# Keys of a group's two halves in the same columns, so that two blocks a group are turned instead of four

## The chip, the cores and the metric

The kernel runs on one core of one Trainium2 chip. The metric is the device time of one execution in microseconds, the median of several runs. A core has TensorE (PE in the profile), VectorE (DVE), ScalarE (ACT), GpSimd (POOL) and a sequencer that mostly issues transfers (SP), and 16 DMA engines that all queues share.

## What is computed

Two layers follow each other, for 8 batches of 3200 rows of 256 columns:

```python
# first layer: z is [B, S, 64], u and v are [B, S, 256]
scores = (1.0 / S) * np.matmul(z, z.transpose(0, 2, 1))
x = u * np.matmul(np.maximum(scores, 0.0) ** 2, v)
# second layer: w_q and w_k are [256, 64], w_out is [256, 256]
wq, wk = x @ w_q, x @ w_k
W_tok = (1.0 / np.sqrt(64)) * np.einsum('bsd,btd->bst', wq, wk)
out = np.maximum(np.einsum('bst,btd->bsd', W_tok, x), 0.0) @ w_out
```

The second layer has no function between its two products, so the kernel computes wk^T x first (a 64 x 256 matrix per batch, called heads here) and then wq times it, which avoids the S x S matrix.

## The kernel before

**Tiles and groups.** A batch's 3200 rows are 25 tiles of 128. They are worked off in 7 groups: six of 512 rows (4 tiles) and a last one of 128 rows (1 tile). For each group PE makes the scores of all 25 tiles against the group's rows (`scores`, L219, two tiles a time into the two banks of one PSUM tile), ACT or DVE takes max and scale (`first_stage`, L243 and L247), POOL or ACT squares (`second_stage`, L260 and L262), and PE accumulates the squares times v (`second_product`, L316). Since the scores are symmetric, some of them are not computed twice: blocks of squares are turned by a DMA transpose (L282) and used for another group. Most matmuls contract over 64 rows, and two of them run side by side, one on the upper 64 rows of the array, one on the lower; `top(r)` names these halves.

**From a finished group to its keys.** `gate` (L353) multiplies the accumulated product by u on DVE and writes x in fp16, laid out so that one DMA transpose (`turn_x`, L377) leaves the columns of tiles 0 and 1 of the group on the upper 64 rows and of tiles 2 and 3 on the lower. `projections` (L394) then multiplies by w_q and w_k together. The weights lie the other way round in the lower half: for tiles 0 and 1 (bank 0 of the PSUM tile) the queries come out on the upper rows and the keys on the lower; for tiles 2 and 3 (bank 1) the keys come out on the upper rows and the queries on the lower. `projections_out` (L407) copies both banks to an fp16 tile `qk` with one ACT copy of 128x512. `turn_keys` (L412) turns all four 128x128 blocks of `qk` by one DMA transpose on SP's queue into `kx`, of which `heads` (L421) uses the half with the keys. `mix` (L457) later multiplies the queries, which it reads from `qk` itself, by the heads of the batch; `proj` and `proj_stage` (L484, L509) multiply by w_out, and the output is stored (L563).

**What sets the order.** The kernel is unrolled and written out by a planner that runs while the program is built. It holds a clock for PE, DVE, ACT and POOL (`clock`), gives every piece of work a cost in microseconds (`give`), and decides by these clocks what PE issues next: second products (`acc_step`), a pair of scores (`use_pair`), or an extra such as keys, heads, mix or projection (`use_keys`, `use_heads`, `use_mix`, `use_proj`). Scores and extras need one of two PSUM slots (`slots`, tag `ps`), which stay closed until the planned end of the copy that empties them. DMA issues on SP are put in a list with a ready time, a due time, an issue cost and a cost on the DMA engines (`move`, `send`; a turned block costs 0.21 there); the ripe one that is due first is sent. The turn of keys becomes ready `SLACK` (1 us) after the copy and is due 10 us after it. Whether ACT or DVE does a first stage, and POOL or ACT a square, is the planner's choice by its clocks. `NAT` is the number of buffers for squares: a pair of tiles may only be made when the pair `NAT` before it has been used up; `lead` (140) sets how far ahead of the second products pairs are wanted.

**The tail.** The last batch's heads go another way for its last groups (`last_gram`, `last_heads`, L577 and L587). After the planned part some steps are written out by hand (L1077 to L1104), among them the projections of the last batch's groups 5 and 6 with their copies (L1096).

Of the kernel before, what the change touches and what calls it, by code (L numbers as in the profile page):

```python
# [9 lines left out]
FP16 = mybir.dt.float16  # L10
# [6 lines left out]
def kernel(  # L17
# [10 lines left out]
    nc = tc.nc  # L28
# [3 lines left out]
    dh = moe_w_q.shape[1]  # L32
    P = 128
# [3 lines left out]
    W = 512  # L37
    HW = W // 2
    widths = [512] * 6 + [128]
# [10 lines left out]
    ALPHA = C1 * float(S) * float(S)  # L50
    FINAL_SCALE = 1.0 / (8.0 * ALPHA * ALPHA * ALPHA)

    NAT = 15
    NX = 7
    NK = 5

# [5 lines left out]
    pk = ctx.enter_context(tc.tile_pool(name="pk", bufs=NK))  # L62
# [3 lines left out]
    psum = ctx.enter_context(tc.tile_pool(name="psum", bufs=2))  # L66
    pat = ctx.enter_context(tc.tile_pool(name="pat", bufs=NAT))
    ptt = ctx.enter_context(tc.tile_pool(name="ptt", bufs=1))
# [6 lines left out]
    def ps_tile(name):  # L75
        return pps.tile([P, 2, W], FP32, tag="ps", name=name)
# [5 lines left out]
    def top(r):  # L82
        return slice(r * dqk, (r + 1) * dqk)
# [3 lines left out]
    zT, vs, us, xs, xTs, qks, ks, hacc, hx, hss, rts, zds = ({} for _ in range(12))  # L87
# [294 lines left out]
    def x_rows(b, gi, n):  # L382
        return xs[b, gi][:, n % 2, :, n // 2, :]
# [3 lines left out]
    def halves(gi):  # L387
        return range((widths[gi] // P + 1) // 2)

    def projections(b, gi, ps):  # L390
        n = min(2, widths[gi] // P)
        for c in range(NC):
            for r in halves(gi):
                nc.tensor.matmul(  # L394
                    out=ps[:, r, 0 : n * P],
                    lhsT=wqk[top(r), c, :, :].rearrange("p t h -> p (t h)"),
                    rhs=xTs[b, gi][top(r), 0:n, c, :],
                    start=(c == 0),
                    stop=(c == NC - 1),
                )  # L400

    def projections_out(b, gi, ps):
        xTs.pop((b, gi))
        n = min(2, widths[gi] // P)
        qks[b, gi] = pq.tile([P, 2, HW], FP16, tag="qk", name="qk")
        nr = len(halves(gi))
        nc.scalar.copy(out=qks[b, gi][:, 0:nr, 0 : n * P], in_=ps[:, 0:nr, 0 : n * P])  # L407

    def turn_keys(b, gi):
        nn = widths[gi] // P  # L410
        ks[b, gi] = pk.tile([P, 4, 2, dh], FP16, tag="kx", name="kx")
        nc.sync.dma_start_transpose(  # L412
            out=ks[b, gi][:, 0:nn, :, :].rearrange("p n a h -> p n (a h)"),
            in_=qks[b, gi][:].rearrange("p r s -> p (r s)")[:, 0 : nn * P],
        )

    def heads(b, gis, ps):
        todo = [(gi, n) for gi in gis for n in range(widths[gi] // P)]
        for i, (gi, n) in enumerate(todo):
            for r in range(2):  # L420
                nc.tensor.matmul(  # L421
                    out=ps[top(i % 2), r, 0:D],
                    lhsT=ks[b, gi][top(r), n, 1 - n // 2, :],
                    rhs=x_rows(b, gi, n)[top(r), :, :],
                    start=(i < 2),
                    stop=(i >= len(todo) - 2),
                )
        for gi in gis:
            del xs[b, gi], ks[b, gi]
# [23 lines left out]
    def mix(b, gi, banks):  # L453
        n = min(2, widths[gi] // P)
        for db in range(ND):
            for r in halves(gi):
                nc.tensor.matmul(  # L457
                    out=banks[r][:, ds(db * n * P, n * P)],
                    lhsT=hss[b][top(r), ds(db * P, P)],
                    rhs=qks[b, gi][top(r), r, 0 : n * P],  # L460
                    start=(db == 0),
                    stop=(db == ND - 1),
                )
# [133 lines left out]
    PE, DVE, ACT, POOL = range(4)  # L597
    clock = [0.0] * 4
    FROM_PE, HOP = 0.27, 0.12

    def give(engine, ready, weight):
        clock[engine] = max(clock[engine], ready) + weight
        return clock[engine] + HOP
# [16 lines left out]
    def at_time(t, fn):  # L620
        later.append((t, fn))

    def move(ready, due, issue, takes, fn, landed=None, may=None):
        moves.append((ready, due, issue, takes, fn, landed, may))
# [29 lines left out]
    def open_slot():  # L654
        slot = slots.pop(0)
        assert slot[0] < 1e9
        clock[PE] = max(clock[PE], slot[0])
        slot[0] = 1e9
        slots.append(slot)
        return slot  # L660

    def close_slot(slot, t):
        slot[0] = t
# [40 lines left out]
    def use_keys(b, gi):  # L704
        slot = open_slot()
        ps = ps_tile("qk")
        projections(b, gi, ps)
        clock[PE] += 0.44 if gi < LASTG else 0.24
        ready = clock[PE] + FROM_PE
        projections_out(b, gi, ps)  # L710
        done = give(ACT, ready, 0.56)
        n = widths[gi] / P
        if b < last or gi < GRAM:
            move(
                done + SLACK, done + 10.0, 1.28, 0.21 * n, lambda: turn_keys(b, gi),
                lambda t: at_time(t, lambda: keys_landed(b, gi)), lambda: len(ks) < NK,
            )
        close_slot(slot, done)
# [3 lines left out]
    def keys_landed(b, gi):  # L722
        keyed.append((b, gi))
        for gis in FIRST_HEADS, range(3, NG if b < last else GRAM):
            if gi in gis and all((b, i) in keyed for i in gis):
                add_extra(clock[PE] + 0.5, "heads", lambda gis=gis: use_heads(b, gis))

    def use_heads(b, gis):
        slot = open_slot()
        ps = ps_tile("hd")  # L730
        heads(b, gis, ps)
        clock[PE] += 0.2 + 0.0547 * sum(widths[gi] // P for gi in gis)
        heads_out(b, ps)
        done = give(DVE, clock[PE] + FROM_PE, 0.7)
        close_slot(slot, done)
        if gis is FIRST_HEADS:
            return
        done = give(DVE, done, 0.35)
        move(done + SLACK, done + 2.0, 0.55, 0.1, lambda: cross_heads(b, 0))
        move(  # L740
            done + SLACK, done + 2.0, 0.55, 0.1, lambda: cross_heads(b, 1),
            lambda t: at_time(t, lambda: crossed(b)),
        )
# [16 lines left out]
    def use_mix(b, gi):  # L760
        slot = open_slot()
        ps = ps_tile("mx")
        mix(b, gi, [ps[:, 0, :], ps[:, 1, :]])
        clock[PE] += 0.22
        mix_out(b, gi, ps)
        done = give(ACT, clock[PE] + FROM_PE, 1.03 if gi < LASTG else 0.3)
        close_slot(slot, done)
        add_extra(done + 0.5, "proj", lambda: use_proj(b, gi))
# [91 lines left out]
    def x_landed(t, b, gi):  # L860
        if b < last or gi < LASTG - 1:
            add_extra(t + (XWAIT if b < last else 0.5), "keys", lambda: use_keys(b, gi))
# [100 lines left out]
    def p_chunk(p):  # L963
        t = [x[2] for x in tiles[2 * p : 2 * p + 2]]
        return max(c for c, (n0, nn) in enumerate(ZCH) for i in t if n0 <= i < n0 + nn) if p < 12 else 3

    def all_used(p):
        return all(x in used for x in tiles[2 * p : 2 * p + 2])
# [33 lines left out]
    while stages or work:  # L1002
# [17 lines left out]
        p = produced[0]  # L1020
        able = p < NPAIR and z_at[p_chunk(p)] <= now and (p < NAT or all_used(p - NAT) and turned_at.get(p - NAT, 0.0) <= now and not out_of.get(p - NAT))
        wanted = able and p * total < (done_acc[0] + lead) * NPAIR
# [40 lines left out]
    def mixed(b, gi, i=None):  # L1063
        if i is None:
            ps = ps_tile("mx")
            banks = [ps[:, 0, :], ps[:, 1, :]]
        else:
            ps = banks = [acc_tile(h, i % 2, "mx")[:] for h in range(len(halves(gi)))]
        mix(b, gi, banks)
        mix_out(b, gi, ps)  # L1070
# [22 lines left out]
    for gi in (LASTG - 1, LASTG):  # L1093
        ps = ps_tile("qq")
        projections(last, gi, ps)
        projections_out(last, gi, ps)  # L1096
# [38 lines left out]
```

## Time and profile before

| | us |
|---|---|
| median of 3 runs | 776.21 |
| the three runs | 772.63, 777.22, 776.21 |
| the profiled execution | 774.39 |
| its span, first to last instruction | 772.6 |
| granted TensorE clock, mean | 0.996 |

The profile has several views. The page gives busy time per engine, the span in 40 slices, the DMA queues, and the chain of work that ended last. The windows view gives for each stretch its length, then for PE, PEld (weight loads), DVE, ACT and POOL the busy time and number of instructions, then the granted clock, the DMA share and GB/s. The list of groups has one row for a line, engine, operation and shape: total busy time, mean nanoseconds of one, and the idle time before them with what ended it. The waits view has who waited for whom: total, times, longest. The timeline has instructions in order of time: start, length, engine, line and what ended an idle time before. A matmul's listed length is that of the whole passage through the array, so neighbouring ones overlap.

### The profile page before, as it was taken

What the parts mean: (1) busy time and instruction counts of PE and PEld (TensorE: products, weight loads), DVE (VectorE), ACT (ScalarE), POOL (GpSimd) and SP (SyncE); (2) the same over time, 40 slices, a digit from 0 to 9 for tenths busy, and PEclk for the clock granted to TensorE, in tenths of its full rate; (3) what the DMA queues carried; (4) which work ended last, traced back from release to release, by engine and by line L of the source; (5) the groups of instructions that cost most, each with busy time, mean ns of one, the idle gap of its engine ahead of it and who ended that gap; (6) DMA issues with size and microseconds to landing.
All of it is one profiled execution on the core that took longest, in us unless ns stands there. A gap on an engine that the chain in (4) does not pass through costs nothing.

```text
span 772.6 us, 28742 instructions
## 1 busy us (share of the span) xinstructions
PE 752.0 (97%) x12707; PEld 653.9 (85%) x12707; DVE 461.9 (60%) x497; ACT 496.9 (64%) x651; POOL 564.2 (73%) x363
## 2 busy tenths in 40 slices
PE   6999999999999999999999999999999999999996
PEld 3788889888888889988898898889988899888884
DVE  5775466555586365655556654755577656566644
ACT  6565666765676656777666666776657566775435
POOL 7996687885888477776788567875787768878740
PEclk9999999999999999999999999999999999999999
DMA  7999999999999999999999999999999999999536
GB/s 196 154 173 154 172 180 176 158 219 205 180 181 171 207 217 181 169 178 223 196 218 155 178 204 199 205 186 170 206 173 194 164 177 207 205 200 171 160 84 232
DMA packets 310094, 142.49 MB, mean 184 GB/s; under 512 B 287440, under 2 KB 291408, under 8 KB 309968
## 3 DMA queue, kind: packets, MB, share of 16 engines
q1 hardware_dynamic: 303056, 124.47, 88.9%
q0 software_dynamic: 6768, 15.98, 15.1%
q8 instruction: 99, 1.62, 0.9%
q14 instruction: 27, 0.22, 0.1%
q10 hardware_dynamic: 144, 0.20, 0.1%
HBM read 59.64 MB, written 26.21 MB: 111 GB/s over the span
## 4 chain that ended last, share of the span: by engine, by line
PE 93%; DMA 2%; DVE 2%; ACT 2%; issue 0%; POOL 0%; DVEq 0%; ACTq 0%
PE acc L316 68%; PE sc L224 13%; PE fo L509 5%; PE qk L394 3%; PE hd L421 2%; PE mx L457 1%; DVE g L247 1%; DMA tt<-at 1%; DMA v_sb<-in_v_dram 1%; PE fo L484 1%; ACT g L243 1%; ACT at L260 0%; DMA z<-in_z_dram 0%; ACT rt L472 0%; PE xtx L577 0%
## 5 line engine op out<-in xcount | busy, mean ns | idle before, releaser
L262 POOL TENSOR_TENSOR at<-g 128x1024 f16<-128x1024 f32 (+1 forms) x279 | 520.2, 1880 | 171.7 <-DVE g L247 123.5
L316 PE MATMUL acc<-v_sb,at 64*128 64x256 f16 x7312 | 493.7, 269 | 3.7 <-DMA v_sb<-in_v_dram 2.3
L247 DVE TENSOR_SCALAR g<-sc 128x1024 f32<-128x1024 f32 (+1 forms) x292 | 348.5, 1207 | 214.0 <-PE sc L224 198.1
L316 PEld LDWEIGHTS <-at 64*128 64x128 f16 x7312 | 386.7, 94 | 57.6 <-issue 4.6
L243 ACT ACTIVATE g<-sc 128x1024 f32<-128x1024 f32 (+2 forms) x176 | 173.1, 988 | 118.1 <-PE sc L224 106.8
L260 ACT ACTIVATE at<-g 128x1024 f16<-128x1024 f32 (+2 forms) x189 | 191.1, 1019 | 18.3 <-DVE g L247 14.7
L224 PE MATMUL sc<-zT 64*128 64x512 f16 x920 | 175.8, 378 | 2.9 <-DVE g L247 2.0
L316 PE MATMUL acc<-v_sb,tt 64*128 64x256 f16 x2304 | 167.4, 269 | 1.7 <-DMA tt<-at 1.3
L316 PEld LDWEIGHTS <-tt 64*128 64x128 f16 x2304 | 123.9, 94 | 18.3 <-DMA tt<-at 1.6
L353 DVE TENSOR_TENSOR x_sb<-acc,u_sb 128x512 f16<-128x512 f32 x92 | 59.1, 684 | 26.2 <-PE acc L316 23.1
L562 ACT ACTIVATE fo<-fo 128x1024 f32<-128x1024 f32 (+2 forms) x44 | 42.7, 980 | 37.3 <-PE fo L509 33.3
L224 PEld LDWEIGHTS <-zT 64*128 64x128 f16 x920 | 55.3, 94 | 13.0 <-issue 8.3
L474 ACT ACTIVATE rt<-mx 128x1024 f16<-128x1024 f32 (+1 forms) x49 | 44.7, 929 | 17.1 <-PE mx L457 17.0
L509 PE MATMUL fo<-wo,rt 64*128 64x256 f16 x668 | 52.2, 269 | 0.2 <-DVE g L247 0.2
L407 ACT CAST qk<-qk 128x512 f16<-128x512 f32 (+1 forms) x54 | 29.2, 540 | 25.5 <-PE qk L394 25.3
L509 PEld LDWEIGHTS <-rt 64*128 64x128 f16 x668 | 36.1, 94 | 3.3 <-issue 0.4
L303 ACT COPY sign<-sign 1x1 f32<-1x1 f32 x95 | 17.3, 182 | 33.1 <-PE acc L316 31.2
L394 PE MATMUL qk<-xT_sb,wqk 64*128 64x256 f16 (+1 forms) x404 | 31.6, 265 | 0.0
L316 PE MATMUL acc<-v_sb,ttl 64*128 64x256 f16 x384 | 27.2, 269 | 0.0
L394 PEld LDWEIGHTS <-wqk 64*128 64x128 f16 x416 | 22.3, 94 | 2.0 <-issue 0.3
L316 PEld LDWEIGHTS <-ttl 64*128 64x128 f16 x384 | 20.5, 94 | 2.7
L526 DVE COPY sign<-sign 1x1 f32<-1x1 f32 x31 | 4.4, 142 | 29.9 <-PE fo L509 29.7
(54 smaller groups left out, 203.7 us busy)
## 6 DMA issues: line engine op xcount, KB each, us to landing
u_sb<-in_u_dram SPq DMA_DIRECT2D x48, 512.0 KB, 4.9
out_dram<-fo SPq DMA_DIRECT2D x45, 512.0 KB, 3.9
v_sb<-in_v_dram POOLq DMA_DIRECT2D x35, 320.0 KB, 6.0
zn<-in_z_dram POOLq DMA_DIRECT2D x7, 400.0 KB, 6.2
tt<-at SPq DMA_TRANSPOSE x144, 4.7
out_dram<-fo SPq DMA_DIRECT2D x6, 256.0 KB, 2.4
u_sb<-in_u_dram SPq DMA_DIRECT2D x8, 128.0 KB, 3.6
hx<-ha SPq DMA_DIRECT2D x16, 64.0 KB, 4.0
```

The source lines that it names most:

```text
L224: nc.tensor.matmul(out=sc[:, h, 0:gw], lhsT=zT[b][top(h), ts(ti, P)], rhs=zT[b][top(h), ds(gs, gw)], start=True, stop=True,)
L243: nc.scalar.activation(out=g[:, hs, 0:w], in_=sc[:, hs, 0:w], func=RELU, scale=GSCALE)
L247: nc.vector.tensor_scalar(out=g[:, hs, 0:w], in0=sc[:, hs, 0:w], scalar1=0.0, scalar2=GSCALE, op0=AOP.max, op1=AOP.mult,)
L260: nc.scalar.square(out=out, in_=g[:, hs, 0:w])
L262: nc.gpsimd.tensor_mul(out=out, in0=g[:, hs, 0:w], in1=g[:, hs, 0:w])
L316: product = nc.tensor.matmul(out=g["acc"][k][:, ds(j * D, D)], lhsT=weights(b, gi, ti, 2 * k + j if whole else 0)[top(r), :], rhs=vs[b][to ...
L353: nc.vector.tensor_mul(out=out, in0=g["acc"][k][:].rearrange("p (m d) -> p m d", d=dh), in1=u2.rearrange("p n (c d) -> p (n c) d", d=dh),)
L394: nc.tensor.matmul(out=ps[:, r, 0 : n * P], lhsT=wqk[top(r), c, :, :].rearrange("p t h -> p (t h)"), rhs=xTs[b, gi][top(r), 0:n, c, :], st ...
L407: nc.scalar.copy(out=qks[b, gi][:, 0:nr, 0 : n * P], in_=ps[:, 0:nr, 0 : n * P])
L474: nc.scalar.activation(out=out, in_=ps[:, 0:nr, 0 : ND * n * P], func=RELU)
L509: product = nc.tensor.matmul(out=ps[:, bank, ds(j * D, D)], lhsT=flat[top(r), ds((dc * n + j) * P, P)], rhs=wo[top(r), dc, :], start=(stag ...
L562: nc.scalar.mul(out=flat_out[:, sl], in_=part, mul=FINAL_SCALE)
```

## The change

The single ACT copy becomes two copies of 64 rows, one for the upper and one for the lower half, and the second writes its two banks in reverse order. So in a full group slot 0 of `qk` holds the queries of both halves and slot 1 the keys of both halves. The transpose takes slot 1 alone, two blocks instead of four, and `kx` has half the size. `heads` and `mix` read the new places. The last, small group copies its one block to slot 1. Both copies of a group go to the same engine, ACT or DVE, whichever the planner's clocks call free first; in the hand-written tail they stay on ACT. The planner costs the pair at 1.17 us (0.3 for the small group) where it had 0.56, and the turn at half of what it was on the DMA engines. `NAT` goes from 15 to 16.

```diff
-    NAT = 15
+    NAT = 16
...
-    def projections_out(b, gi, ps):
+    def projections_out(b, gi, ps, on_act=True):
         xTs.pop((b, gi))
         n = min(2, widths[gi] // P)
         qks[b, gi] = pq.tile([P, 2, HW], FP16, tag="qk", name="qk")
-        nr = len(halves(gi))
-        nc.scalar.copy(out=qks[b, gi][:, 0:nr, 0 : n * P], in_=ps[:, 0:nr, 0 : n * P])
+        copy = nc.scalar.copy if on_act else nc.vector.tensor_copy
+        if widths[gi] == W:
+            copy(out=qks[b, gi][top(0), :, :], in_=ps[top(0), :, 0 : n * P])
+            copy(out=qks[b, gi][top(1), ::-1, :], in_=ps[top(1), :, 0 : n * P])
+        else:
+            copy(out=qks[b, gi][:, 1, 0 : n * P], in_=ps[:, 0, 0 : n * P])
...
     def turn_keys(b, gi):
-        nn = widths[gi] // P
-        ks[b, gi] = pk.tile([P, 4, 2, dh], FP16, tag="kx", name="kx")
+        nn = min(2, widths[gi] // P)
+        ks[b, gi] = pk.tile([P, 2, 2, dh], FP16, tag="kx", name="kx")
         nc.sync.dma_start_transpose(
             out=ks[b, gi][:, 0:nn, :, :].rearrange("p n a h -> p n (a h)"),
-            in_=qks[b, gi][:].rearrange("p r s -> p (r s)")[:, 0 : nn * P],
+            in_=qks[b, gi][:, 1, 0 : nn * P],
         )
...
-                    lhsT=ks[b, gi][top(r), n, 1 - n // 2, :],
+                    lhsT=ks[b, gi][top(r), n % 2, 1 - n // 2, :],
...
-                    rhs=qks[b, gi][top(r), r, 0 : n * P],
+                    rhs=qks[b, gi][top(r), 0 if widths[gi] == W else 1, 0 : n * P],
...
         ready = clock[PE] + FROM_PE
-        projections_out(b, gi, ps)
-        done = give(ACT, ready, 0.56)
-        n = widths[gi] / P
+        takes = 1.17 if widths[gi] == W else 0.3
+        on_act = max(clock[ACT], ready) < max(clock[DVE], ready)
+        projections_out(b, gi, ps, on_act)
+        done = give(ACT if on_act else DVE, ready, takes)
+        n = min(2, widths[gi] // P)
```

## The prediction

> **What bounds the kernel now.** I read the page first: busy time, the slices, the DMA queues and the chain that ended last.
>
> ```profile
> span 772.6 us, 28742 instructions
> ...
> PE 752.0 (97%) x12707; PEld 653.9 (85%) x12707; DVE 461.9 (60%) x497; ACT 496.9 (64%) x651; POOL 564.2 (73%) x363
> ...
> DMA  7999999999999999999999999999999999999536
> DMA packets 310094, 142.49 MB, mean 184 GB/s; under 512 B 287440, under 2 KB 291408, under 8 KB 309968
> q1 hardware_dynamic: 303056, 124.47, 88.9%
> HBM read 59.64 MB, written 26.21 MB: 111 GB/s over the span
> PE 93%; DMA 2%; DVE 2%; ACT 2%; issue 0%; POOL 0%; DVEq 0%; ACTq 0%
> ```
>
> Two resources look full: PE, busy for 97% of the span, and the DMA engines, nine tenths in nearly every slice. The chain decides: 93% of it is PE and 2% DMA. ACT (64%) and DVE (60%), which the change loads, have room on average. Next I split the span in start, body and tail with the windows view, and asked whom PE waits for in the body.
>
> ```profile
> 0.00:20.00 20.00, 12.45 (x117) 7.89 (x119) 11.01 (x13) 12.85 (x14) 15.36 (x23) 0.91 0.78 193
> 20.00:740.00 720.00, 714.45 (x12270) 626.41 (x12266) 437.14 (x467) 470.15 (x610) 544.82 (x336) 1.00 1.08 185
> 740.00:772.60 32.60, 25.09 (x331) 19.58 (x325) 13.77 (x19) 13.87 (x29) 3.99 (x6) 0.95 0.50 167
> ```
>
> ```profile
> PE sc L224 <- DVE g L247: 1.6, 3, 1.0
> PE acc L316 <- DMA tt<-at: 1.3, 1, 1.3
> PE acc L316 <- POOL at L262: 0.7, 1, 0.7
> ```
>
> In the windows the first number after the stretch is its length, the second PE's busy time; a wait has its total, its times and its longest. In the body PE is idle for 720.00 - 714.45 = 5.55 us; start and tail have 7.55 and 7.51 us. Of the body's idle time only 1.3 us is put down to a transfer, in one wait. The DMA share of 1.08 there (queues overlapping on the same engines) costs PE almost nothing as the order stands.
>
> Busy PE can hide short gaps, since one matmul's 0.269 us covers the next one's start. So I worked out how much PE time the matmuls need when they stream.
>
> ```profile
> 745.43 3.00 PE L316 MATMUL acc<-v_sb,at 64*128 64x256 f16 x52
> L316 PE MATMUL acc<-v_sb,at 64*128 64x256 f16 x7312 | 493.7, 269 | 3.7 <-DMA v_sb<-in_v_dram 2.3 <-POOL at L262 0.7 <-ACT sign L303 0.4
> L316 PE MATMUL acc<-v_sb,tt 64*128 64x256 f16 x2304 | 167.4, 269 | 1.7 <-DMA tt<-at 1.3 <-DVE x_sb L353 0.3
> L316 PE MATMUL acc<-v_sb,ttl 64*128 64x256 f16 x384 | 27.2, 269 | 0.0
> L224 PE MATMUL sc<-zT 64*128 64x512 f16 x920 | 175.8, 378 | 2.9 <-DVE g L247 2.0 <-ACT g L243 0.2
> L509 PE MATMUL fo<-wo,rt 64*128 64x256 f16 x668 | 52.2, 269 | 0.2 <-DVE g L247 0.2
> L394 PE MATMUL qk<-xT_sb,wqk 64*128 64x256 f16 (+1 forms) x404 | 31.6, 265 | 0.0
> L457 PE MATMUL mx<-qk,hs 64*128 64x256 f16 (+1 forms) x208 | 19.8, 266 | 0.5 <-ACT qk L407 0.5
> L421 PE MATMUL hd<-x_sb,kx 64*64 64x256 f16 x382 | 13.9, 273 | 0.0
> L484 PE MATMUL fo<-wo,rt 128*128 128x256 f16 x66 | 8.5, 273 | 1.4 <-DVE fo L557 1.3
> ```
>
> Row one: 52 matmuls, two at a time on the two halves of the rows, take 3.00 us, of which the last pair's 0.27; (3.00 - 0.27) / 25 = 0.109 us a pair. The 256-column groups have (7312 + 2304 + 384 + 668 + 404 + 208) / 2 = 5640 pairs, 615 us; the scores 460 pairs of twice the columns, 100 us; heads 13.9 us; the tail's projections (L484) 8.5 and three smaller groups some 6 us. Together about 744 us. So 772.6 - 744 = 28.6 us of the span is not streaming, 20.6 of it the visible idle time and about 8 hidden. The change adds and removes no matmul, so it can gain at most 5.55 + 8 = 13.6 us in the body, and only where a wait goes; 7.7 us are 1%.
>
> **The change part by part.** *The second copy.* One copy of 128x512 per full group becomes two of 64 rows by 512 columns each, both on the engine that the planner calls free first.
>
> ```profile
> L407 ACT CAST qk<-qk 128x512 f16<-128x512 f32 x47 | 27.4, 583 | 24.9 <-PE qk L394 24.7
> L434 DVE COPY ha<-hd 128x512 f32<-128x512 f32 x8 | 5.5, 689 | 4.0 <-PE hd L421 3.9
> L189 POOL CAST wqk<-wk 64x256 f16<-64x256 f32 x2 | 0.8, 406 | 0.0
> L120 POOL CAST zd<-z 128x384 f16<-128x384 f32 x1 | 0.5, 498 | 1.5 <-DMA z<-in_z_dram 1.5
> L120 POOL CAST zd<-z 128x448 f16<-128x448 f32 x1 | 0.6, 570 | 0.0
> ```
>
> No row has 64 rows by 512 columns on ACT or DVE. If the time went with the rows, a copy would cost half of 0.583 = 0.29 us and the pair nothing more than now; if it goes with the columns, 0.583 on ACT and, by the nearest DVE row that reads PSUM, 0.689. The only casts with 64 rows are POOL's: 0.406 us for 256 columns, while its 128-row casts fall by 0.072 us per 64 columns, to about 0.35 at 256. Half the rows were no cheaper, so I take the upper end: the pair costs 1.17 us on ACT (+0.58) and 1.38 on DVE (+0.80 over the old copy; 0.21 over the planner's 1.17). With 48 full groups that is 28 to 38 us more work on two engines that are idle for some 276 and 311 us. [...]
>
> What lies on the path? Until both copies are done, one of the two score slots (the PSUM pair "ps") stays shut 0.6 to 0.8 us longer, and ACT or DVE starts its next item later. PE's cover is the second product, which needs no slot: the planner chooses it when no slot is open. The cover is missing where no row of it is ready; today's price for that is the row PE sc <- DVE g, 1.6 us in 3 waits. Bounds for the body: 0 if all is covered, 46 x 0.6 = 28 us if none is (of the 47 copies in the row above one is in the tail); near the lower end by that row, I take +1.0 us. Behind a copy on DVE stand the next L247 and the gate L353; behind one on ACT the next L243, L260, sign L303. The planner moves both clocks by 1.17, so only DVE's 0.21 is unknown to it; at most 24 copies x 0.21 = 5 us, counted within those bounds. The keys themselves are not urgent: they are due 10 us after the copy, and SP's transpose is sent 1 us (SLACK) after the planned end, which holds DVE's 0.21. If that cover went, SP would stand, with the loads of u and the turned blocks behind it.
>
> *The turn.* 12 blocks fewer in each of 7 batches and 8 in the last: 92 blocks of 128x128.
>
> ```profile
> L412 SPq DMA_TRANSPOSE kx<-qk x53: 1123/1275/3088, 68.5 to 735.5; - x53
> 83.64 0.61 PE L316 MATMUL acc<-v_sb,tt 64*128 64x256 f16 x8 [1.34 <-DMA tt<-at]
> ```
>
> The number of transposes stays 53, and SP's issue time falls little: one-block turns are among these 53, yet the shortest is 1.123 us against a median of 1.275, so up to 0.15 us each, 8 us of SP's time in all, on no path that PE shows. The DMA work of a block: the program turns about 2110 blocks (1344 of the products, 400 of x, 191 of keys, 175 of z), 287440 small packets, 136 a block. Queue 1's packets average 0.889 x 772.6 x 16 / 303056 = 36 ns, so 136 x 36 / 16 = 0.31 us at most (large packets raise that mean), and 0.21 in the planner. 92 blocks are 19 to 28 us of DMA time, 2.5 to 3.7%. On PE's path it can return what PE waits for transfers in the body: 0 to 1.3 us seen. I take -1.3, the one late turned block, since it falls at 83.6 us, when key turns are running (from 68.5 us). [...]
>
> *The planner.* Turns are costed at half, pairs may run 16 instead of 15 ahead (NAT), and the copies move between ACT and DVE. NAT rarely decides: the lead of 140 products lets pairs run 140 x 460 / 5000 = 13 ahead of the mean. I cost it at nothing, within the body's bounds: the 13.6 us above as gain, and as loss some waits of the kind listed, like the longest now (1.3 us) a few times. The order after the first key copy will differ nearly everywhere. The other edits (heads and mix read other columns of the same tiles, the small group's copy stays one of 128x128) issue the same instructions as before: nothing, with one answer.
>
> *The tail.* Here PE has no second product to hide behind.
>
> ```profile
> 750.77 0.59 ACT L407 CAST qk<-qk 128x512 f16<-128x512 f32 x1
> 751.40 0.39 PE L457 MATMUL mx<-qk,hs 64*128 64x256 f16 x4 [0.46 <-ACT qk L407]
> 751.73 2.14 PE L577 MATMUL xtx<-xd 128*128 128x256 f16 x18
> 756.19 0.75 ACT L407 CAST qk<-qq 128x512 f16<-128x512 f32 x2 [0.89 <-PE qq L394]
> 756.83 2.21 ACT L472 ACTIVATE rt<-mx 128x512 f16<-128x512 f32 x4
> ```
>
> At 751.4 PE already waits 0.46 us for group 4's copy, and everything after stands behind it in order: +0.6 (ACT) to +0.8 (DVE). At 756.19 the copies of groups 5 and 6 stay on ACT; the first becomes two, and the four activations that PE's last products need start directly behind: +0.59. Bounds 0 (time by rows) to 1.4; I take +1.2.
>
> **Sum.** +1.0 - 1.3 + 0 + 1.2 = +0.9 us. The profiled execution took 774.39 us (1.8 outside its span) and lies 1.8 below the median of the three runs, 776.21, inside their 772.63 to 777.22. 774.4 + 0.9 = **775.3 us**.
>
> **Rivals.**
> *The slot becomes the bound (slower).* The longer hold makes PE wait before the next scores where all ready rows of the second product are used up. For: PE has already 3 such waits of up to 1.0 us, and two slots serve scores, keys, heads, mix and projections. Against: PE's idle time before the scores is 1.6 us in 720. It decides from about 13 of the 46 copies exposed (13 x 0.6 = 8 us); with 20, +12: 786 us.
> *The freed DMA time pays (faster).* Turned blocks land earlier, rows are ready earlier and the gaps close. For: the DMA share of 1.08 in the body. Against: one DMA wait of 1.3 us. All visible idle time of the body gone: 774.4 + 1.2 - 5.55 = 770; over 1% needs about 4 us of the hidden as well: 766 us.
> *The turn does not get cheaper.* If a transpose's time goes by instruction and not by block, the -1.3 is lost and the copies remain: 774.4 + 2.2 = 776.6 us. For: the narrow spread of issue times, 1.123 to 1.275. Against: 136 packets for each block.
>
> **How the numbers follow.** The forecast 0.46; the turn not cheaper 0.22; the slot 0.24; DMA pays 0.08. A measurement of this kernel can tell about 1% from no change (its own three runs spread 0.6%). Forecast and dearer turn lie within 1% of 774 to 776: 0.68; slower 0.24; faster 0.08. The range reaches down to 768, between the two ends of the DMA rival, and up to 785, just under the slot rival's price, since half of that rival's cases are milder than its 20 exposed copies; some 0.05 is left out below and 0.13 above.
>
> **What would show it.** Copies: two L407-like rows per group, 64x512, 0.58 on ACT and 0.69 on DVE; 0.29 would mean time by rows. Turn: kx transposes still 53, small packets down by 92 x 136 = 12500, DMA share of the body down by 0.03. Body: PE idle near 5 us, waits of sc for g or qk still under 3 us; 10 us or more is the slot rival. Tail: the stretch from 740 longer by about a microsecond. I am wrong if PE's idle time in the body falls by several microseconds, or if it grows in places that no copy touches: then the planner's new order did it, a term that I set to nothing.

## The result, and the profile after

The changed kernel takes 782.82 us (median of 6 executions) against 775.77 for the kernel before in the same comparison: 1.0085 times as long, 95% interval 1.0055 to 1.0114. The forecast was 775.3 us, no change; the change is a small loss. Executions more than 1.5% above the fastest one of the same kernel are left out of the ratios and ranges here (794.91 us of the change, 785.71 of e3, 789.66 of e4, four of e9 from 788.9 to 789.6, and 2786.82 of e8), so that the spreads of the change, e3, e4 and e9 are if anything larger than given.

The executions of the changed kernel lie far apart, from 776.6 to 786.5 us; those of before lie within 5 us. The profiled execution is the fastest one, 776.62 us with a span of 774.5, 1.9 us longer than the span of before, so most of the loss is not in it. The page of after, the three windows and PE's waits in the body:

```profile
span 774.5 us, 28772 instructions
...
DMA packets 298317, 139.47 MB, mean 180 GB/s; under 512 B 275664, under 2 KB 279632, under 8 KB 298192
...
q1 hardware_dynamic: 291280, 121.46, 83.3%
```

```profile
0.00:20.00 20.00, 13.11 (x105) 8.01 (x106) 10.95 (x13) 12.05 (x13) 15.30 (x23) 1.00 0.77 189
20.00:740.00 720.00, 714.34 (x12264) 617.92 (x12265) 471.02 (x525) 464.46 (x589) 556.39 (x347) 1.00 1.03 181
740.00:774.50 34.50, 25.81 (x343) 20.12 (x338) 13.93 (x19) 14.39 (x29) 4.25 (x6) 0.95 0.47 157
```

```profile
PE sc L224 <- DVE g L247: 2.8, 5, 0.8
PE mx L463 <- DVE g L247: 0.6, 1, 0.6
...
PE sc L224 <- DVE qk L409: 0.2, 1, 0.2
```

The DMA work fell: 11776 small packets fewer (92 blocks of 128; the prediction had counted 136 a block), queue 1 from 88.9 to 83.3% of the span, the body's DMA share from 1.08 to 1.03 (0.03 was forecast), and the 1.3 us wait for a turned block is gone. PE shows no gain from it: its idle time in the body is 5.66 us where it was 5.55. So 5.6 points less of queue 1's share bought no time that shows. What the copies cost, in the list of groups of after by shape:

```profile
L408 DVE CAST qk<-qk 64x512 f16<-64x512 f32 x36 | 24.6, 682 | 28.7 <-PE qk L394 28.6
L409 DVE CAST qk<-qk 64x512 f16<-64x512 f32 x36 | 25.0, 695 | 0.5
L408 ACT CAST qk<-qk 64x512 f16<-64x512 f32 x11 | 6.4, 578 | 6.2 <-PE qk L394 6.1
```

The time goes with the columns, not the rows: 0.68 and 0.70 us on DVE and 0.58 on ACT are the times of 128 rows of 512 columns (0.69 on DVE in e4, 0.58 on ACT in before), while the small group's 128 rows of 128 columns took 0.29 on DVE and 0.26 on ACT in this trace. 36 of the 47 planned pairs went to DVE, 1.38 us each where the planner counts 1.17. PE's wait for a copy's slot in the body is one of 0.2 us.

So this trace shows the copies hidden in the body, the turns halved, and a span 1.9 us longer, of which the tail has 1.2 (shown further down). The rest of the loss had to be looked for in the order of the work and in slower executions.

### The profile page after: what moved, and what is told of

The parts are those of the page before. It is cut to its first block, busy times and chain, and to the rows that moved or that the text cites. A ratio compares the mean times of both kernels' runs of the same rounds, so it can differ in the third digit from the quotient of the medians.

```text
span 774.5 us, 28772 instructions
## 1 busy us (share of the span) xinstructions
PE 753.3 (97%) x12707; PEld 646.0 (83%) x12707; DVE 495.9 (64%) x555; ACT 490.9 (63%) x629; POOL 575.9 (74%) x375
## 3 DMA queue, kind: packets, MB, share of 16 engines
q1 hardware_dynamic: 291280, 121.46, 83.3%
## 4 chain that ended last, share of the span: by engine, by line
PE 92%; DVE 3%; ACT 1%; issue 1%; DMA 1%; POOL 0%; DVEq 0%; ACTq 0%; POOLq 0%
PE acc L316 67%; PE sc L224 13%; PE fo L515 5%; PE qk L394 3%; DVE g L247 2%; PE hd L427 2%; PE mx L463 1%; DMA v_sb<-in_v_dram 1%; PE fo L490 1%; ACT at L260 0%; DMA z<-in_z_dram 0%; ACT g L243 0%; PE xtx L583 0%; ACT rt L478 0%; POOL at L262 0%
## 5 line engine op out<-in xcount | busy, mean ns | idle before, releaser
L262 POOL TENSOR_TENSOR at<-g 128x1024 f16<-128x1024 f32 (+1 forms) x291 | 532.1, 1845 | 160.1 <-DVE g L247 107.0
L247 DVE TENSOR_SCALAR g<-sc 128x1024 f32<-128x1024 f32 (+1 forms) x277 | 329.7, 1205 | 148.3 <-PE sc L224 136.9
L243 ACT ACTIVATE g<-sc 128x1024 f32<-128x1024 f32 (+2 forms) x191 | 188.1, 990 | 125.3 <-PE sc L224 120.5
L260 ACT ACTIVATE at<-g 128x1024 f16<-128x1024 f32 x177 | 183.1, 1042 | 28.6 <-DVE g L247 25.8
L224 PE MATMUL sc<-zT 64*128 64x512 f16 (+1 forms) x920 | 180.5, 380 | 4.1 <-DVE g L247 3.2
L316 PE MATMUL acc<-v_sb,tt 64*128 64x256 f16 x2304 | 164.1, 269 | 0.0
L408 DVE CAST qk<-qk 64x512 f16<-64x512 f32 x36 | 24.6, 682 | 28.7 <-PE qk L394 28.6
L316 PE MATMUL acc<-v_sb,ttl 64*128 64x256 f16 x384 | 29.2, 269 | 0.0
L409 DVE CAST qk<-qk 64x512 f16<-64x512 f32 x36 | 25.0, 695 | 0.5
```

The lines of the kernel that those rows point to most:

```text
L224: nc.tensor.matmul(out=sc[:, h, 0:gw], lhsT=zT[b][top(h), ts(ti, P)], rhs=zT[b][top(h), ds(gs, gw)], start=True, stop=True,)
L243: nc.scalar.activation(out=g[:, hs, 0:w], in_=sc[:, hs, 0:w], func=RELU, scale=GSCALE)
L247: nc.vector.tensor_scalar(out=g[:, hs, 0:w], in0=sc[:, hs, 0:w], scalar1=0.0, scalar2=GSCALE, op0=AOP.max, op1=AOP.mult,)
L260: nc.scalar.square(out=out, in_=g[:, hs, 0:w])
L262: nc.gpsimd.tensor_mul(out=out, in0=g[:, hs, 0:w], in1=g[:, hs, 0:w])
L316: product = nc.tensor.matmul(out=g["acc"][k][:, ds(j * D, D)], lhsT=weights(b, gi, ti, 2 * k + j if whole else 0)[top(r), :], rhs=vs[b][to ...
```

## Experiments

Ratios are against the kernel before on the same chip, with 95% intervals. Two theories stood at first: that the second copy holds the PSUM slot and PE waits for it (the copies), and that the planner's new order is worse (the order). The program's order can be held fixed while the work is changed, since the planner decides by its own costs; e2 has the order of before on PE, SP and POOL, and e4 that of e3, but for the size of the key turns.

**e1_again: the changed kernel once more.**

> The changed kernel once more, for its spread and a second trace. Both theories: 1.006 to 1.012 times the time before. Theory of the order (the planner's new order of work brings waits that differ from one execution to the next): spans from about 774 to 784 us again, far wider than the 5 us of the kernel before. Theory of the copies (the second copy of each group holds its PSUM slot 0.6 to 0.8 us longer, and PE waits for it): the same excess in every execution, so a narrow spread.

Measured 784.0 us, 1.0146 (1.0114 to 1.0178), 781.1 to 789.5. The wide spread is there again, and the loss is larger. Its trace has a span of 779.0 us, and waits that the first trace of after does not have or has much shorter (there 1.3 us for the exchange, 0.6 for mix, none of PE for keys or x):

```profile
DVE hs L454 <- DMA hx<-ha: 5.3, 2, 4.2
PE mx L463 <- DVE g L247: 3.2, 2, 2.5
PE hd L427 <- DMA kx<-qk: 1.0, 1, 1.0
PE qk L394 <- DMA xT_sb<-x_sb: 0.7, 1, 0.7
```

```profile
20.00:740.00 720.00, 709.68 (x12180) 615.00 (x12176) 467.62 (x522) 459.81 (x581) 551.28 (x345) 1.00 1.03 181
```

PE is idle for 10.3 us in this body, 4.8 more than in before, and PE's three waits above add up to 4.9. None of them is for a copy of queries and keys.

The timeline of the longest: the two transfers that exchange the halves of the heads, DVE's sum that needs them, the first stages behind it, and PE's mix.

```profile
233.11 2.14 SPq L156 DMA_TRANSPOSE zT<-zd  x1
235.34 1.18 SPq L449 DMA_DIRECT2D hx<-ha  x2
240.80 0.43 DVE L454 TENSOR_TENSOR hs<-ha,hx 128x256 f16<-128x256 f32 x1 [4.24 <-DMA hx<-ha]
241.14 2.35 DVE L247 TENSOR_SCALAR g<-sc 128x1024 f32<-128x1024 f32 x2
242.41 0.39 PE L463 MATMUL mx<-qk,hs 64*128 64x256 f16 x4 [2.50 <-DVE g L247]
```

The sum stands in DVE's queue ahead of the landing; DVE is idle for 4.24 us, no first stage frees a slot, and PE waits 2.50 us. DVE had come to the sum at 236.6 us, 1.2 us after the exchange was issued. In the first trace of after, the same sum of the same program does not wait:

```profile
230.92 1.23 SPq L156 DMA_TRANSPOSE zT<-zd  x1
232.24 1.48 SPq L449 DMA_DIRECT2D hx<-ha  x2
235.58 0.92 DVE L454 TENSOR_TENSOR hs<-ha,hx 128x256 f16<-128x256 f32 x1
```

There the exchange went out 3.1 us earlier. In e1 it stood behind transposes on SP's queue whose issue took longer (the last of them 2.14 us against 1.23). In the kernel before, the same pair of rows is 7.4 us apart and nobody waits:

```profile
236.39 1.18 SPq L443 DMA_DIRECT2D hx<-ha  x2
243.82 0.41 DVE L448 TENSOR_TENSOR hs<-ha,hx 128x256 f16<-128x256 f32 x1
```

**e2_old_order: the work of the change in the order of before.**

```diff
-    NAT = 16
+    NAT = 15
...
-        on_act = max(clock[ACT], ready) < max(clock[DVE], ready)
-        projections_out(b, gi, ps, on_act)
-        done = give(ACT if on_act else DVE, ready, takes)
-        n = min(2, widths[gi] // P)
+        projections_out(b, gi, ps)
+        done = give(ACT, ready, 0.56)
+        n = widths[gi] / P
```

> The work of the change in the order of before: two copies of 64 rows (all on ACT) and two turned blocks, but the planner's costs and NAT of before, so every engine issues in the order of before, with one more ACT copy per full group. Theory of the order: 0.997 to 1.003, of which 1 us is the tail's two longer copies. Theory of the copies: 1.006 or more, since the longer hold is not even planned for.

Measured 787.58 us, 1.0174 (1.0160 to 1.0188), all four executions within 0.7 us. The copies do cost time where the planner doesn't know of them. Its waits, and one of them:

```profile
PE sc L224 <- ACT qk L409: 5.9, 21, 0.7
```

```profile
138.83 0.71 PE L316 MATMUL acc<-v_sb,at 64*128 64x256 f16 x10
139.19 0.58 ACT L409 CAST qk<-qk 64x512 f16<-64x512 f32 x1
139.83 0.39 PE L224 MATMUL sc<-zT 64*128 64x512 f16 x2 [0.28 <-ACT qk L409]
```

The ten products before the scores stream for 5 x 0.109 = 0.55 us, so the scores could start at 139.38; they start at 139.83. The list shows 0.28 us of these 0.45, since the products' last passage covers the rest. At that size, 21 such waits make 9.5 us of the 13.5, an estimate; eight waits of PE for the same copy before other work list 2.1 us, and the tail's two copies make 1.2 more.

**e3_nat15 and e4_new_order_old_work: one order, both kinds of work.** The first is the change with NAT 15. The second has its order, but one copy of 128x512 and four turned blocks:

```diff
-        nc.scalar.copy(out=qks[b, gi][:, 0:nr, 0 : n * P], in_=ps[:, 0:nr, 0 : n * P])
+        copy = nc.scalar.copy if on_act else nc.vector.tensor_copy
+        copy(out=qks[b, gi][:, 0:nr, 0 : n * P], in_=ps[:, 0:nr, 0 : n * P])
...
-        projections_out(b, gi, ps)
-        done = give(ACT, ready, 0.56)
-        n = widths[gi] / P
+        takes = 1.17 if widths[gi] == W else 0.3
+        on_act = max(clock[ACT], ready) < max(clock[DVE], ready)
+        projections_out(b, gi, ps, on_act)
+        done = give(ACT if on_act else DVE, ready, takes)
+        n = min(2, widths[gi] // P)
```

> The change with NAT at 15 instead of 16. If the 16th buffer is what changes the order for the worse: within 0.3% of before. If the order is bad for the costs of the copies and turns: 1.005 to 1.012, as the change. Theory of the copies: 1.008.

> The order of the kernel with NAT 15 and the planner's new costs, but with the work of before: one copy of 128x512 (on the engine that this order gives it) and four turned blocks. PE, SP and POOL issue in the same order as in that kernel. Theory of the order: 1.005 to 1.012, like the kernel with NAT 15. Theory of the copies: 0.997 to 1.003, since the copy is short again.

Measured 1.0034 (1.0011 to 1.0057), 773.9 to 784.4, and 1.0045 (1.0018 to 1.0071), 774.3 to 784.4. With the order the same, the second copies and the halved turns together change nothing that can be told; these two runs do not separate a cost of the one from a gain of the other. The old work in a new order is slower than before and spreads just as widely. The theory of the copies falls for planned copies. The excess is a little below what the theory of the order had said; the rest came with NAT 16, the only thing in which e1 (1.0146) differs from e3.

**What in the order?** The planner puts a consumer where it expects its transfer to have landed: the end of its DMA clock plus 4.0 us (LANDS). The change halves the cost of a key turn in that clock. Running the planner of each kernel gives its own figures: from issue to expected landing x takes 8.0 us before and 7.3 after, all SP transfers 7.55 and 7.30. The measured medians did not follow for x:

```profile
xT_sb<-x_sb SPq DMA_TRANSPOSE x56, 4.8
```

```profile
xT_sb<-x_sb SPq DMA_TRANSPOSE x56, 5.2
```

(before, then after). For the keys both went down, the planner's figure from 6.9 to 6.7 us and the measured median from 4.7 to 4.2. For the exchange of the heads the planner's figure went up, from 5.9 to 6.3, so the long wait of e1 does not come from an earlier expected landing of the exchange itself; it went out late, as shown above. So a second theory was put against chance: work is planned closer to its transfers (the DMA clock), or any order other than that of before costs as much (any new order).

**e5_turn_at_four and e6_lands_5: the change with honest or later landings.** In e5 `n = min(2, widths[gi] // P)` in `use_keys` goes back to `n = widths[gi] / P`; in e6 `LANDS = 4.0` becomes 5.0.

> The change, except that the planner goes on costing a turn of keys at four blocks (0.84 us) on the DMA engines, though two are turned. Theory of the DMA clock (with the turn at half, the planner expects transfers to land earlier than they do, and puts the work that needs them, above all DVE's sum of the heads after the exchange, ahead of the landing): 0.998 to 1.004, and the time from the issue of the heads' exchange to DVE's sum back from 2.4 to 8 us to 4.6 us and more, as before. Theory of any new order (an order other than the one of before costs about as much whatever changed it): 1.005 to 1.015.

> The change, with the planner expecting every SP transfer to land 5.0 us after its place in the DMA clock instead of 4.0. Theory of the DMA clock: 0.998 to 1.005 and a spread near that of before. Theory of any new order: 1.005 to 1.015.

Measured 1.0030 (1.0011 to 1.0049), 774.6 to 780.2, and 1.0024 (1.0004 to 1.0044), 772.9 to 779.7. One number in the planner takes back most of the loss, though on another chip than e1's; on e1's chip e14 has 1.0044. But e5's trace still has one long wait for the exchange, whose sum DVE reached 1.6 us after the issue, so its distances were not back as far as expected. It also shows what came with that wait:

```profile
146.13 0.43 DVE L454 TENSOR_TENSOR hs<-ha,hx 128x256 f16<-128x256 f32 x1 [4.76 <-DMA hx<-ha]
147.75 0.61 PE L224 MATMUL sc<-zT 64*128 64x512 f16 x2 [3.13 <-DVE g L247]
```

```profile
146.00:149.00 3.00, 1.16 (x8) 0.57 (x9) 2.87 (x4) 1.14 (x2) 0.10 (x1) 0.74 1.08 259
149.00:152.00 3.00, 3.00 (x38) 2.57 (x37) 1.21 (x2) 1.13 (x2) 3.00 (x2) 0.69 1.04 208
152.00:155.00 3.00, 3.00 (x58) 2.89 (x55) 2.17 (x3) 2.08 (x4) 2.54 (x2) 1.00 1.28 193
```

From 146 to 152 us, with the end of PE's pause in it, the granted clock is 0.74 and then 0.69, and PE gets through 38 matmuls in 3 us where it does 58 at 1.00. If the fall belongs to the pause, this late transfer cost more than the wait that the list puts down to it. For the 2.50 us wait in e1 no such fall is to be seen in the clocks: the first 20 us have 0.91 and the stretch from 740 us on 0.96 in both traces, and the mean of the whole execution is 0.996 in e1 and 0.994 in e5, where 6 us at 0.7 make some 0.002, an estimate.

**e7_before_turn_at_two and e8_before_copy_060: the kernel before with one planner number moved.** e7 halves the cost of the turn, e8 moves the copy's 0.56 to 0.60; all work is that of before.

> The kernel before, all its work kept (one copy on ACT, four turned blocks), only the planner's cost of the turn on the DMA engines halved. Theory of the DMA clock: 1.005 to 1.015 with a wide spread, since the planner's clock runs ahead of the transfers. Theory of the copies: no change, 0.998 to 1.002. Theory of any new order: 1.003 to 1.015 as well, so this run alone doesn't tell these two apart; the next one does.

> The kernel before, all its work kept, only the planner's cost of the key copy on ACT moved from 0.56 to 0.60 us, which changes the order without touching the DMA clock's costs. Theory of the DMA clock: 0.998 to 1.003 and a narrow spread. Theory of any new order: 1.003 to 1.015.

Measured 1.0049 (1.0023 to 1.0075), 775.1 to 785.0, and 1.0050 (1.0026 to 1.0073), 777.7 to 781.1. The medians do not tell the theories apart: a neutral change of order costs 0.5% too, against the expectation. The spreads do: 9.9 us against 3.4 (of 12 and 6 executions). And only e7's trace has PE waiting for a transfer:

```profile
PE hd L421 <- DMA kx<-qk: 1.7, 1, 1.7
```

**e9_sum_on_pool: the late sum out of DVE's queue.** `nc.vector.tensor_add` of the heads' sum becomes `nc.gpsimd.tensor_add`, in the order of the change.

> The change in its own order, except that the sum of the heads after their exchange is added by POOL and not by DVE, so that a late exchange no longer stands ahead of the first stages in DVE's queue (it then stands ahead of the squares in POOL's). Theory that this one wait makes most of the excess and the spread: 1.001 to 1.006, with the spread halved. Theory that the order places many things too close to the transfers: 1.008 to 1.015, as the change.

Measured 1.0070 (1.0040 to 1.0099), 775.2 to 783.6. That wait is one of several, not most of it. The trace, of an execution of 788.91 us, has many:

```profile
PE hd L427 <- DMA kx<-qk: 9.8, 6, 4.7
```

**e10_old_order_one_copy and e11_new_order_one_copy: halved turns without a second copy.** A full group's projections write queries and keys to their places at once, and one copy of 128x512 moves both banks; e10 also has e2's edits of `NAT` and of the planner's costs:

```diff
-            for r in halves(gi):
-                nc.tensor.matmul(
-                    out=ps[:, r, 0 : n * P],
-                    lhsT=wqk[top(r), c, :, :].rearrange("p t h -> p (t h)"),
+            for half in range(2 if widths[gi] == W else 0):
+                for r in halves(gi):
+                    nc.tensor.matmul(
+                        out=ps[top(half), 0 if half == r else 1, 0 : n * P],
+                        lhsT=wqk[top(r), c, half, :],
...
+            copy(out=qks[b, gi][:], in_=ps[:, :, 0 : n * P])
```

> The order of before (costs and NAT of before), two blocks turned, and one copy of 128x512: the projections of a full group are made as 16 products of 64 rows and 64 columns, four at a time, that write queries and keys straight to the places which the change gives them. Against before only the key turns are half as large, and the projections take as long. Theory that freed DMA time pays: 0.993 to 0.998. Theory that it is hidden: 0.998 to 1.002. If small products cost more than four at a time: up to 1.01.

> The change's own order on PE, SP and POOL, NAT 16, two blocks turned, but one copy per full group in the way of the kernel with one copy and the old order; the planner still counts 1.17 us for it. Theory of the order: 1.006 to 1.015, since the order is the change's, with the second copies gone. Theory of the copies: 0.997 to 1.003.

Measured 1.0125 (1.0106 to 1.0144) and 1.0178 (1.0135 to 1.0221). The small products are not free. Weight loads of the projections in before, then in e10:

```profile
L394 PEld LDWEIGHTS <-wqk 64*128 64x128 f16 x416 | 22.3, 94 | 2.0 <-issue 0.3
```

```profile
L395 PEld LDWEIGHTS <-wqk 64*64 64x64 f16 x768 | 17.4, 106 | 10.2 <-issue 10.0
```

That is 8.2 us more idle time before them, where the tiles go over from 64*128 to 64*64 (in the body 44 waits of up to 0.2 us, 9.3 us in all); about as much as e10 lost (10.4 us). What the engine does in that time these rows do not show. What is left shows no gain from halved turns in the order of before. e11 has the same products and is therefore no clean test. Its spread is 10.7 us, and late keys and sums are in its trace:

```profile
DVE hs L462 <- DMA hx<-ha: 6.6, 4, 2.9
PE hd L435 <- DMA kx<-qk: 2.7, 1, 2.7
```

The mean granted clock of this execution is 0.996, with 1.00 in the first 20 us and 0.98 from 740 us on; worked out from these, its body lacks some 2 us of full clock, an estimate, about what a fall like e5's takes.

**e12_before_lands_3: the kernel before, landings expected 1 us earlier.** `LANDS = 4.0` becomes 3.0.

> The kernel before, all its work and costs kept, except that the planner expects every SP transfer to land 3.0 us after its place in the DMA clock instead of 4.0. Theory of the DMA clock: the same fault by another edit, so 1.004 to 1.02, the executions spread over 8 us or more, and PE or DVE waits for kx, xT or hx appear, which the trace of before does not have. Theory of any new order: about 1.005 with a spread of at most 6 us, as with the copy cost of 0.60.

Measured 1.0044 (1.0017 to 1.0070), 774.3 to 783.1, a spread of 8.9 us. Another edit that brings consumers nearer to their transfers, the same signature. Its profiled execution is the fastest, and PE's list there has no transfer. DVE has one wait of the expected kind, for the last batch's exchange, with PE busy meanwhile:

```profile
743.70 0.42 DVE L451 TENSOR_TENSOR ha<-ha,hx 128x256 f32<-128x256 f32 x1 [2.67 <-DMA hx<-ha]
```

**e13_turn_at_four_nat15 and e14_turn_at_four_lands_5: the remedy in other orders.** The change with the turn costed at four blocks, with NAT 15, or with LANDS 5.0.

> The change with the turn of keys costed at four blocks and NAT 15, its work unchanged. Theory of the DMA clock: 1.000 to 1.004 with a spread of at most 6 us, where the kernel with NAT 15 and the halved cost ran from 773.9 to 785.7. Theory of any new order: anything from 1.003 to 1.015, the spread no guide.

> The change with both remedies, the turn costed at four blocks and landings expected 1 us later. Theory of the DMA clock: 0.998 to 1.003 and a spread of at most 5 us. Theory of any new order: 1.003 to 1.015.

Measured 1.0010 (0.9994 to 1.0027), 774.4 to 778.5, and 1.0044 (1.0028 to 1.0059), 777.6 to 778.7. Both are narrow, as expected; the second's median is higher than expected. In these runs an order with ample margins is steady, not necessarily fast.

**e15_split_copies: the two copies on ACT and DVE at once.** Turn at four blocks, `nc.scalar.copy` for the upper rows and `nc.vector.tensor_copy` for the lower, planned with `done = max(give(ACT, ready, 0.58), give(DVE, ready, 0.7))`.

> The change with the turn costed at four blocks, and the two copies of a full group side by side, the upper half on ACT and the lower on DVE, planned so; in the tail too. The slot is shut for 0.7 us instead of 1.17 to 1.38. If the longer hold costs what is left: 0.996 to 1.001. If the hold is hidden wherever the planner knows of it: 1.000 to 1.004, less only the tail's 1 us.

Measured 1.0195 (1.0169 to 1.0221), 788.1 to 791.3. They did not run at once: in the trace the second copy starts when the first has ended. Why the program orders them so was not looked into.

```profile
DVE qk L409 <- ACT qk L408: 55.5, 39, 3.7
...
PE sc L224 <- DVE qk L409: 4.5, 14, 0.7
```

The slot was shut for 0.58 + 0.70 us and more where 0.70 was planned: e2's fault again, though the waits listed for it make only a part of the 14.8 us. A true split was not tried, so what the planned hold still costs is bounded only by e3 against e4.

The spreads side by side, lowest to highest execution in us, with the number of executions where it is under 8; the planner's own mean time from issue to expected landing is 6.5 to 7.3 us in the first row and 7.5 to 8.5 in the second:

| expected landings | kernels and spreads |
|---|---|
| earlier than in before | after 9.8 (5), e1 8.4 (6), e3 10.5, e4 10.1, e7 9.9, e9 8.4, e11 10.7 (6), e12 8.9 |
| as in before, or later | before 4.6 to 5.7, e2 0.7 (4), e5 5.6, e6 6.8, e8 3.4 (6), e10 1.1 (5), e13 4.1, e14 1.1, e15 3.2 (5) |

## Why the prediction was wrong, point by point

- **The bound was read rightly.** PE sets the time, it can gain little, and freed DMA time is worth little: the DMA work of 92 blocks went and PE shows no gain (e3 against e4, the body's idle time).
- **The copies were priced rightly** (by columns; 1.17 and 1.38 us a pair, measured 1.16 and 1.38), and that the second product covers the longer hold held where the planner knew of it. The +1.0 us for the body is less than e3 against e4 can show or rule out. DVE took 36 pairs, not at most 24.
- **The tail's +1.2 us held.** PE's wait for group 4's copy went from 0.46 to 1.04 us, and the stretch from the first xtx product to the end, which holds the other long copy, from 772.6 - 751.73 = 20.9 to 774.5 - 753.03 = 21.5:

```profile
752.71 0.39 PE L463 MATMUL mx<-qk,hs 64*128 64x256 f16 x4 [1.04 <-ACT qk L409]
753.03 2.14 PE L583 MATMUL xtx<-xd 128*128 128x256 f16 x18
```

- **The turn's -1.3 us** was wrongly booked: that wait is gone from the trace of after, but others stand in its place and PE's idle time in the body is the same. One late block of one execution is no property of the order. A block's packets were put 6% too high (136 for 128), and the DMA share that it frees too low (0.03 for 0.05).
- **The step that failed is "The planner. ... I cost it at nothing".** The new order, at NAT 15, costs 0.5% with the old work in it (e4), and the prediction's own last sentence names that sign: in e1 PE's idle time in the body grew by 4.8 us in places that no copy touches. "NAT rarely decides" was wrong too: e1 and e3 differ in nothing else, and take 1.0146 and 1.0034. The rest has two parts. The halved turn cost is a claim on landings: the prediction weighed it as DMA time freed, not as consumers placed earlier. And "the keys themselves are not urgent" looked at when the turn is due, not at what stands behind the landing: heads on PE, in the program's order. PE or DVE waits of over 0.5 us for keys, x or the exchange are in the traces of after, e1, e4, e7, e9, e11 and e12, and in e5 and e6, which spread most of their row; they are in none of before, e2, e8, e10, e13, e14 and e15. Of the first row only e3's trace, of one of its fastest executions, has none so long.

```profile
PE qk L394 <- DMA xT_sb<-x_sb: 2.3, 1, 2.3
```

That last row is e4's. Ordinary re-ordering is the other part: e8 and e14 lose 0.4 to 0.5% with honest landings, e13 0.1%. The order of before was a favourable one among those tried, which the profile of before alone could not show.
- **The slot rival** was the right mechanism in the wrong place: it decides where the hold is not planned (e2 +13.5 us, e15 +15), not where it is.
- **The base** was one execution of a kernel whose executions agree. The changed one's do not, and a sum against one trace cannot forecast that.

What stays open: why NAT 16 with the halved cost loses 0.9 to 1.5% and NAT 15 with it 0.3%; which of the late waits makes how much of a slow execution, since each trace shows one execution, and around one of them, e5's, the granted clock was 0.74 and 0.69 for 6 us; and why even the fastest executions of the change lose, 776.6 and 781.1 us in its two comparisons against 772.6 and 772.7. That the spread follows the expected landings is shown over the seventeen entries of the table (eleven different orders); that it is these late waits and nothing else is argued from the traces that have them.

## What to carry to other kernels

In a kernel whose order comes from a model, a cost in the model is a claim about when things are ready: lowering it moved consumers of keys and x nearer to their transfers here, even though the work saved was hidden anyway. Change work and order one at a time, since holding the order fixed tells in two runs which of them made the difference. Look at the spread of the executions beside their median; here consumers placed close to their transfers showed in the spread where medians did not tell, and the fastest trace showed few of them.

## What was not expected of the hardware

Copies of 64 rows by 512 columns took as long as copies of 128 (0.58 and 0.58 us on ACT, 0.68 to 0.70 and 0.69 on DVE). Sixteen products of 64 rows and 64 columns took 0.63 us in e10's trace where eight of 64 by 128 took 0.60 in before's, but the weight loads stood idle for up to 0.2 us before them, 44 times in the body. One and the same exchange went out 3.1 us later on SP's queue in one execution (e1) than in another of the same program (after), and the sum behind it waited 4.24 us in the one and not at all in the other. Around the end of a pause of PE that is listed with 3.13 us (e5) the granted clock was 0.74 and then 0.69 for 6 us; with pauses of 2.50 us (e1) and 2.3 us (e4) the mean of the whole execution was 0.996, with 0.91 in the first 20 us and 0.96 from 740 us on, and 0.999, which leaves no room for such a fall.
